# A shuffle taken out of one step into the next, and one weight difference moved from VectorE to GpSimd

## The chip, the cores and the metric

The kernel runs on one core of a Trainium2 chip. The time is the device time of that core in microseconds, as the median of several runs. The profile is of one execution of the program, taken by the hardware profiler.

## What is computed

An RWKV-6 attention over 4 batches, 8 heads, 768 tokens and a head size of 48, followed by a feed-forward layer with SiLU. All data is fp32.

```python
# r, k, v, w: (4, 8, 768, 48), u: (8, 48)
for t in range(S):
    kt, vt, rt, wt = (k[:, :, t], v[:, :, t], r[:, :, t], w[:, :, t])
    cur = np.einsum('bhd,bhe->bhde', u[None] * kt, vt)
    y[:, :, t] = np.einsum('bhd,bhde->bhe', rt, state + cur)
    state = wt[:, :, :, None] * state + np.einsum('bhd,bhe->bhde', kt, vt)
...
x = y.transpose(0, 2, 1, 3).reshape(B * S, H * D)     # (3072, 384)
h = x @ w_in                                          # w_in (384, 2048)
out = (h * (1.0 / (1.0 + np.exp(-h)))) @ w_out        # w_out (2048, 384)
```

## The kernel before

The work is cut into 12 units. A unit is 128 tokens of two batches (NB = 2); units 0 and 1 are the first 128 tokens of the four batches, units 2 and 3 the next 128, and so on. The order of all instructions is written out by hand: each engine has a queue that it works through in the order in which the program emits, and an engine that waits holds up all that is queued behind it.

**Attention of a unit.** The 128 x 128 scores of tokens against earlier tokens are built over seven levels l = 0 to 6. At level l, blocks of 2^l tokens meet their neighbours: `score_products` multiplies queries with keys on TensorE (L669), `keep_masked` (L679) copies the valid part from PSUM into `score` on VectorE, `grow_queries` (L607, VectorE) and `grow_keys` (L625, GpSimd) multiply queries and keys with the products of w for the next level. `prepare` (L737) makes queries for a next level in a second buffer ahead of time, so that `burst` can run two levels' products on TensorE at once: levels 3 and 4, later 5 and 6. The transposed inputs are made by `turn` (L360, VectorE), the products of w by `product` (L408, GpSimd) and a first growth of the keys by `grow_own` (L634, GpSimd).

**Scores within a block of 8.** From unit 3 on, the first three levels of scores are dot products made on GpSimd (`block_bonus`, L487) and summed on VectorE (`block_sum`, L521). `block_move` stores the sums in DRAM and loads them back with tokens on partitions (SP's queue, L540 and L543). `block_spread` copies them to `block_both` on ScalarE (L548, L550) and reverses the partitions of the second batch within groups of 32 on VectorE (L551, a stream shuffle in place). `block_write` (L557) copies `block_both` into `score` under a mask, twice on VectorE. Units 0 to 2 do the like for pairs of tokens with `bonus_spread` and `bonus_write` (L578, L584).

**Then** the keys are turned back (`turn_k`, L781), the state is applied (`y_state`, L794), the scores are applied to v (`y`, L807), and `update` renews the state: TensorE L821, GpSimd L826 (the old state times the decay), VectorE L835. `move_x` (L857) brings the result into the layout of the feed-forward layer by DMA.

**Feed-forward layer.** `up` multiplies with w_in (L925, 12 matmul records for each of 8 m) and applies SiLU on ScalarE (L934). Unit 0 uses a plain `down` (L947, copied out on VectorE by L951). From unit 1 on `down` is a fast 2 x 2 block product in seven quarters (`quarter`, L991, with additions on VectorE by L1000 that also free its PSUM buffers), which needs sums of the activations (`sums`, L973, VectorE: four operations for each of four m) and four differences of the weights, which `weight_sums` makes once: t1 = b12 - b11, t2 = b22 - t1, t3 = b22 - b12, and at last b21 = b21 - t2. The four quarters of w_out are 8 x 192 = 1536 elements on each of 128 partitions; t3 lies in `own[:, 2]` and is read by the quarter with number 3. The weight pieces that are put together at the start are added by GpSimd (L241).

**Order around the change.** For unit 2 the order is written out. Its part with `weight_sums(2)`:

```python
do((burst, 2, 5), (keep_level, 2, 5), (keep_level, 2, 6), (go_on, 2, 6), (up, 1, 6), (bonus_spread, 2), (bonus_write, 2),
   (load_values, 3), *both(turn_k, 2), (weight_sums, 2), (up, 1, 7), (sums, 1, 2))
do((sums, 1, 3), *both(y_state, 2), *both(y, 2), *both(update, 2), ...
```

On GpSimd the instruction before `weight_sums(2)` is thus the last of `grow_keys` in `go_on(2, 6)`, and the one after it the first of `update`. From unit 3 on, `mix` gives 13 groups of attention steps, and between the groups steps of `downs(i - 2)` and `ups(i - 1)` are put in. The groups that hold the block sums' last steps:

```python
[*at(first, *move), *at(later, (block_spread, i), (block_write, i))],
[(burst, i, 5), (keep_level, i, 5), *at(first, (block_spread, i)), (keep_level, i, 6), (go_on, i, 6),
 *at(first, (block_write, i))],
```

Here `first` is unit 3 and `later` the units 4 to 11. In unit 3 the spreading stands ahead of `keep_level(i, 6)` and `go_on(i, 6)` (which holds `grow_queries` of level 6), and the writing behind them.

Of the kernel before, what the change touches and what calls it, by code (L numbers as in the profile page):

```python
# [15 lines left out]
ALU = mybir.AluOpType  # L16
# [22 lines left out]
def kernel(  # L39
# [11 lines left out]
    nc = tc.nc  # L51
# [282 lines left out]
    for b in range(NB):  # L334
        for x in range(2):
            nc.vector.tensor_single_scalar(out=own_mask[:, b, :, x:x + 1], in_=first[0], scalar=tok[:, x, b:b + 1],
                                           op=ALU.is_equal)
# [118 lines left out]
    block_both = spare[:, at:at + NB * H * BLK].rearrange("p (b h s) -> p b h s", b=NB, h=H)  # L456
# [89 lines left out]
    def block_spread(i):  # L546
        flat = block_both.rearrange("p b h s -> p b (h s)")
        nc.scalar.copy(out=flat[:, 0], in_=block_diag[0])  # L548
        for g in range(4):
            nc.scalar.copy(out=flat[(3 - g) * 32:(4 - g) * 32, 1], in_=block_diag[1][g * 32:(g + 1) * 32])  # L550
        nc.vector.stream_shuffle(out=flat[:, 1], in_=flat[:, 1], mask=list(range(31, -1, -1)))  # L551

    def block_write(i):

        shape = [128, NB, NP, L // BLK, BLK]
        for e in range(2):
            nc.vector.copy_predicated(out=score[:, i % NSC, e].rearrange("p (b q) (i s) -> p b q i s", b=NB, s=BLK),  # L557
                                      mask=block_mask[:, :, None].to_broadcast(shape),
                                      data=block_both[:, :, e::2][:, :, :, None, :].to_broadcast(shape))
# [307 lines left out]
    def mix(i):  # L867
# [16 lines left out]
        def start(j):  # L884
# [11 lines left out]
                  [(keep_level, i, 4), (go_on, i, 4), *at(first, (make_block_mask,), *sum_steps(i, 2), *bonus_steps(i, 6))],  # L896
                  [(prepare, i, 5), (reverse_v, i), *at(first, *bonus_steps(i, 7))],
# [3 lines that stand above are left out]
                  [*at(later and ahead, *early)],  # L901
                  [*at(i < len(units) - NB, *both(turn_k, i)), *at(ahead, *turns(i + 1))],
# [59 lines left out]

    def weight_sums(which):
        out, one, two = ((t1, b12, b11), (t2, b22, t1), (t3, b22, b12), (b12, b21, t2))[which]
        nc.vector.tensor_tensor(out=out, in0=one, in1=two, op=ALU.subtract)

    def sums(i, m):

# [91 lines left out]
    for m in range(1, 4):  # L1060
# [11 lines left out]
              2: [(down, 0, 0, 1), (odd_ones, 2), (start_keys, 2, nc.gpsimd, True), (grow_queries, 2, 0), *blocks[3:6]],  # L1072
              3: [(up, 1, 3), (start_keys, 2, nc.gpsimd, False), (reverse_v, 2), *blocks[6:9]], 4: [(level, 2, 1), (up, 1, 4), *blocks[9:12]],
              5: [(down, 0, 0, 2), (up, 1, 5), (weight_sums, 0)]}
    for m in range(6):
        do((piece, 10 + m), *others[m])
    rounding.close()
    second.append(ctx.enter_context(tc.tile_pool(name="po", bufs=1, space=bass.MemoryType.PSUM)))

    blocks = block_loads(4)  # L1080
    do(*blocks[0:2], (level, 2, 2), (prepare, 2, 3), (weight_sums, 1), (down, 0, 1, 0), (down, 0, 0, 3), (down, 0, 1, 1),
       (sums, 1, 0), (bonus, 2, 0), (bonus_sum, 2, 0))
    do(blocks[2], (burst, 2, 3), (keep_level, 2, 3), (keep_level, 2, 4), (go_on, 2, 4), (prepare, 2, 5), (bonus, 2, 1),
       (bonus, 2, 2), (down, 0, 1, 2), (bonus_sum, 2, 1), (load_rk, 3), (load_u,), (sums, 1, 1), *blocks[3:7], (down, 0, 1, 3))
    do((burst, 2, 5), (keep_level, 2, 5), (keep_level, 2, 6), (go_on, 2, 6), (up, 1, 6), (bonus_spread, 2), (bonus_write, 2),
       (load_values, 3), *both(turn_k, 2), (weight_sums, 2), (up, 1, 7), (sums, 1, 2))
    do((sums, 1, 3), *both(y_state, 2), *both(y, 2), *both(update, 2),
       (move_x, 2),
# [47 lines left out]
```

## Time and profile before

| | us |
|---|---|
| median of 3 runs (lowest, highest) | 635.92 (635.87, 636.47) |
| the profiled execution, in all | 636.54 |
| its span | 634.8 |
| PE busy | 620.5 (98%) |
| PEld busy | 561.6 (88%) |
| DVE busy | 434.4 (68%) |
| POOL busy | 373.7 (59%) |
| ACT busy | 185.8 (29%) |

PE is TensorE's matmuls, PEld its weight loads, DVE VectorE, POOL GpSimd, ACT ScalarE, SP the queue that issues the DMAs. Starts are given in us from the begin of the span. The granted clock of TensorE is 0.997 of full speed in the profiled execution. A timeline line gives the start, the length, the engine, the source line, the operation with its output and inputs, the number of instructions merged, and in brackets the idle time of the engine ahead of it with what ended it.

### The profile page before, as it was taken

How to read it: one execution, taken by the hardware profiler on the slowest of the kernel's cores; microseconds unless marked ns; L12 is line 12 of the kernel's file. 1: busy time of each engine (PE TensorE's matmuls, PEld its weight loads, DVE VectorE, ACT ScalarE, POOL GpSimd, SP SyncE). 2: the span in 40 equal slices, each digit the busy share in tenths (PEclk: the TensorE clock that was granted, in tenths of full speed). 3: DMA queues.
4: the chain of work that ended last, by engine and by line, in shares of the span. 5: the costliest groups of instructions: out<-in, count | busy, mean ns of one | idle time of the engine just before them, and what ended most of it. 6: DMA issues, size and time to landing. Idle time of an engine off the chain costs nothing.

```text
span 634.8 us, 12253 instructions
## 1 busy us (share of the span) xinstructions
PE 620.5 (98%) x4574; PEld 561.6 (88%) x4574; DVE 434.4 (68%) x750; ACT 185.8 (29%) x377; POOL 373.7 (59%) x421
## 2 busy tenths in 40 slices
PE   8999999999888999999999999999999999999997
PEld 7888876889788899899889889989989989989997
DVE  7879779885593696696587596497597587561031
ACT  5798881202310321221221221221131122120120
POOL 6998298569469278478278378468458558500000
PEclk9999999999998999999999999999999999999999
DMA  9966864533353643543443442453353222100000
GB/s 216 290 152 167 190 176 50 112 73 65 81 71 55 128 65 52 126 64 51 111 67 52 110 72 49 96 87 51 79 102 53 47 62 52 34 0 26 26 1 25
DMA packets 203292, 53.75 MB, mean 85 GB/s; under 512 B 186465, under 2 KB 194657, under 8 KB 203233
## 3 DMA queue, kind: packets, MB, share of 16 engines
q1 hardware_dynamic: 201648, 52.39, 40.7%
q10 hardware_dynamic: 1584, 0.59, 0.5%
q8 instruction: 36, 0.59, 0.4%
q14 instruction: 24, 0.19, 0.1%
HBM read 43.67 MB, written 5.31 MB: 77 GB/s over the span
## 4 chain that ended last, share of the span: by engine, by line
PE 80%; POOL 9%; DMA 4%; DVE 3%; SPq 2%; issue 1%; ACT 1%; POOLq 0%; DVEq 0%; ACTq 0%
PE p_h L925 36%; PE p_o L991 27%; PE p_sc L669 4%; PE p_m L807 3%; PE p_m L947 2%; PE p_m L669 2%; PE p_m L794 2%; DMA tokens_w<-in_w_dram 2%; POOL ruk L487 2%; POOL tk L625 2%; POOL tw L408 2%; DMA u_bc<-in_u_dram 1%; POOL tk L634 1%; PE p_m L781 1%; PE p_sc L821 1%
## 5 line engine op out<-in xcount | busy, mean ns | idle before, releaser
L925 PE MATMUL p_h<-xt,w_in_sb 128*128 128x256 f32 x1152 | 258.1, 382 | 0.7 <-POOL tk L649 0.7
L925 PEld LDWEIGHTS p_h<-xt,w_in_sb 128*128 128x128 f32 x1152 | 215.9, 190 | 32.6 <-POOL tk L649 0.9
L934 ACT ACTIVATE gt<-p_h 128x512 f32<-128x512 f32 x90 | 53.6, 596 | 248.2 <-PE p_h L925 248.1
L625 POOL TENSOR_TENSOR tk<-tk,tw 128x256 f32<-128x256 f32 x126 | 86.9, 711 | 60.1 <-ACT tk L595 31.3
L991 PE MATMUL p_o<-own,temps 128*128 128x192 f32 x528 | 90.5, 331 | 5.8 <-DVE temps L1000 3.7
L991 PEld LDWEIGHTS p_o<-own,temps 128*128 128x128 f32 x528 | 87.6, 193 | 7.2 <-DVE temps L1000 4.6
L991 PE MATMUL p_o<-w_out_sb,gt 128*128 128x192 f32 x508 | 87.4, 328 | 0.0
L991 PEld LDWEIGHTS p_o<-w_out_sb,gt 128*128 128x128 f32 x508 | 82.7, 190 | 0.9 <-issue 0.4
L487 POOL TENSOR_TENSOR ruk<-tokens_rk 128x768 f32<-128x768 f32 (+1 forms) x36 | 56.3, 1574 | 39.4 <-DMA tokens_rk<-in_k_dram 28.2
L408 POOL TENSOR_TENSOR tw<-tw 128x256 f32<-128x256 f32 (+6 forms) x83 | 45.0, 542 | 52.2 <-DVE tw L360 48.3
L973 DVE TENSOR_TENSOR temps<-gt 128x256 f32<-128x256 f32 x84 | 54.7, 651 | 18.3 <-ACT gt L934 18.3
L595 ACT COPY tk<-tk 128x256 f32<-128x256 f32 x51 | 20.6, 403 | 101.6 <-POOL tk L625 71.9
L607 DVE TENSOR_TENSOR tr<-tr,tw 128x512 f32<-128x512 f32 x62 | 47.6, 768 | 3.7 <-POOL tk L625 1.1
L679 DVE COPY_PREDICATED score<-mask,p_sc 128x512 f32<-128x512 int8 x60 | 42.1, 753 | 10.9 <-PE p_sc L669 10.0
L669 PEld LDWEIGHTS p_sc<-tr,tk 48*128 48x128 f32 x496 | 30.4, 187 | 10.1 <-issue 6.6
L669 PE MATMUL p_sc<-tr,tk 48*128 48x128 f32 x496 | 36.5, 285 | 0.7 <-POOL tk L625 0.7
L521 DVE TENSOR_REDUCE block_sums<-ruk 128x4 f32<-128x192 f32 (+1 forms) x54 | 27.1, 542 | 7.5 <-POOL ruk L487 7.5
L1000 DVE TENSOR_TENSOR ob<-p_o,partial 128x192 f32<-128x192 f32 x22 | 7.9, 358 | 35.4 <-PE p_o L991 35.4
L1000 DVE TENSOR_TENSOR temps<-p_o,partial 128x192 f32<-128x192 f32 x22 | 7.9, 358 | 34.9 <-PE p_o L991 24.7
L557 DVE COPY_PREDICATED score<-spare 128x1024 f32<-128x1024 int8 x18 | 30.6, 1752 | 0.3
L991 PE MATMUL p_o<-w_out_sb,temps 128*128 128x192 f32 x176 | 30.4, 326 | 0.0
L487 POOL TENSOR_TENSOR tokens_rk<-tokens_rk,tokens_w 128x192 f32<-128x192 f32 (+1 forms) x36 | 29.4, 838 | 1.4
(170 smaller groups left out, 825.9 us busy)
## 6 DMA issues: line engine op xcount, KB each, us to landing
w_out_sb<-in_moe_w_in_dram SPq DMA_DIRECT2D x6, 768.0 KB, 8.1
tokens_rk<-in_r_dram SPq DMA_DIRECT2D x9, 384.0 KB, 4.5
tokens_rk<-in_k_dram SPq DMA_DIRECT2D x9, 384.0 KB, 5.5
tokens_w<-in_w_dram SPq DMA_DIRECT2D x9, 384.0 KB, 6.4
w_out_sb<-in_moe_w_out_dram SPq DMA_DIRECT2D x4, 768.0 KB, 6.8
own<-in_moe_w_out_dram SPq DMA_DIRECT2D x4, 768.0 KB, 5.2
xt<-yt SPq DMA_DIRECT2D x60, 48.0 KB, 2.0
raw<-in_w_dram SPq DMA_DIRECT2D x80, 32.0 KB, 2.4
```

The costliest lines, as they stand in the source:

```text
L408: engine.tensor_tensor(out=up, in0=t[:, :, 0::2], in1=t[:, :, 1::2], op=ALU.mult)
L487: mul = lambda out, one, two: nc.gpsimd.tensor_tensor(out=out, in0=one, in1=two, op=ALU.mult)
L521: add = lambda out, have: nc.vector.tensor_reduce(out=out, in_=have, axis=mybir.AxisListType.X, op=ALU.add)
L557: nc.vector.copy_predicated(out=score[:, i % NSC, e].rearrange("p (b q) (i s) -> p b q i s", b=NB, s=BLK), mask=block_mask[:, :, None].to_ ...
L607: nc.vector.tensor_tensor(out=odd, in0=odd, in1=tw[i][l][:, :, 0::2][:, :, :, None].to_broadcast([128, Q, L >> (l + 1), c]), op=ALU.mult)
L625: nc.gpsimd.tensor_tensor(out=out, in0=have, in1=odd_products(i, l, b, *blocks), op=ALU.mult)
L669: nc.tensor.matmul(bass.AP(tensor=s_p.tensor, offset=s_p.offset, ap=[s_p.ap[0], [apart * L // 2, 2], [1, L // 2]]), lhsT=tk[i][rows, X[l % ...
L679: nc.vector.copy_predicated(out=dst, mask=masks[l][:, :, None].to_broadcast([128, NB, NP, ni, c]), data=sc[e].rearrange("p (b q) (i c) -> ...
L925: nc.tensor.matmul(p_h[:, a, :], lhsT=w_in_sb[:, c, f * 128:(f + 1) * 128], rhs=xt[i][:, c, :], start=(c == 0), stop=(c == KC - 1))
L934: nc.scalar.activation(out=gt[i, m], in_=p_h, func=AF.Silu)
L973: nc.vector.tensor_tensor(out=out, in0=one, in1=two, op=op)
L991: nc.tensor.matmul(p, lhsT=left(f), rhs=right[:, f, :], start=(f == 0), stop=(f == FH - 1))
```

## The change

The stream shuffle is taken out of `block_spread` and put at the begin of `block_write`. The third call of `weight_sums` (which = 2, the difference t3) is issued to GpSimd, the other three stay on VectorE. Nothing is computed differently.

```diff
@@ block_spread, block_write
         nc.scalar.copy(out=flat[:, 0], in_=block_diag[0])
         for g in range(4):
             nc.scalar.copy(out=flat[(3 - g) * 32:(4 - g) * 32, 1], in_=block_diag[1][g * 32:(g + 1) * 32])
+
+    def block_write(i):
+
+        flat = block_both.rearrange("p b h s -> p b (h s)")
         nc.vector.stream_shuffle(out=flat[:, 1], in_=flat[:, 1], mask=list(range(31, -1, -1)))
-
-    def block_write(i):
 
         shape = [128, NB, NP, L // BLK, BLK]
         for e in range(2):
@@ weight_sums
     def weight_sums(which):
         out, one, two = ((t1, b12, b11), (t2, b22, t1), (t3, b22, b12), (b12, b21, t2))[which]
-        nc.vector.tensor_tensor(out=out, in0=one, in1=two, op=ALU.subtract)
+        (nc.gpsimd if which == 2 else nc.vector).tensor_tensor(out=out, in0=one, in1=two, op=ALU.subtract)
```

## The prediction

> **What bounds the kernel now.** I began with the busy times of the page, which say where to look for idle time:
>
> ```profile
> PE 620.5 (98%) x4574; PEld 561.6 (88%) x4574; DVE 434.4 (68%) x750; ACT 185.8 (29%) x377; POOL 373.7 (59%) x421
> ```
>
> TensorE is the bound of the whole, so an edit on another engine moves the end only through TensorE's few gaps. The timeline of PE from 95 to 250 us shows them (columns: start us, length us, what, and in brackets the idle time before it and its releaser):
>
> ```profile
> 137.35 5.47 PE L991 MATMUL p_o<-own,temps 128*128 128x192 f32 x32 [1.27 <-DVE temps L1000]
> ...
> 172.11 1.24 PE L781 MATMUL p_m<-ident,tk 128*128 128x128 f32 x8 [1.60 <-DVE score L679]
> ...
> 190.46 2.87 PE L991 MATMUL p_o<-own,temps 128*128 128x192 f32 x16 [2.00 <-DVE temps L1000]
> ...
> 195.43 4.55 PE L991 MATMUL p_o<-own,temps 128*128 128x192 f32 x16 [2.10 <-DVE partial L1000]
> ```
>
> Both edits lie ahead of these gaps; behind 195.43 the only gap noted up to 250 us is 0.45 us, and the chain of waits is PE almost alone. So **the time is set by when VectorE lets the product at 195.43 start**. Backwards from there: its buffer is freed by L1000 (195.03), queued behind L521 (193.60), which waits for GpSimd; GpSimd works from 179.75 to 193.53 with no idle noted, and began when VectorE had transposed w of unit 4 (L360, 178.37). VectorE has no idle between 171.12 and 190.05. One step further back, the timelines of DVE and then of POOL:
>
> ```profile
> 117.30 0.47 DVE L973 TENSOR_TENSOR temps<-gt,spare 128x256 f32<-128x256 f32 x1
> ...
> 118.82 0.55 DVE L951 COPY ob<-p_m 128x384 f32<-128x384 f32 x1
> ...
> 122.54 2.50 DVE L584 COPY_PREDICATED score<-own_mask,both_b 128x1024 f32<-128x1024 int8 x2
> 124.93 2.58 DVE L965 TENSOR_TENSOR own<-w_out_sb 128x1536 f32<-128x1536 f32 x1
> 127.44 1.25 DVE L973 TENSOR_TENSOR temps<-gt 128x256 f32<-128x256 f32 x1
> ...
> 132.33 1.30 DVE L360 STREAM_TRANSPOSE tw<-raw 128x512 f32<-128x512 f32 x2
> ...
> 171.12 0.22 DVE L551 STREAM_SHUFFLE spare<-spare 128x64 f32<-128x64 f32 x1
> 171.25 1.33 DVE L679 COPY_PREDICATED score<-mask,p_m 128x512 f32<-128x512 int8 x2
> 172.47 0.68 DVE L607 TENSOR_TENSOR tr<-tr,tw 128x512 f32<-128x512 f32 x1
> 173.07 2.49 DVE L557 COPY_PREDICATED score<-spare 128x1024 f32<-128x1024 int8 x2
> ```
>
> ```profile
> 116.30 1.19 POOL L625 TENSOR_TENSOR tk<-tk,tw 128x256 f32<-128x256 f32 x2
> 124.66 3.75 POOL L826 TENSOR_TENSOR state<-state,tw 128x512 f32<-128x512 f32 x2 [7.17 <-PE p_m L794]
> 133.72 1.04 POOL L408 TENSOR_TENSOR tw<-tw 128x512 f32<-128x512 f32 x1 [5.31 <-DVE tw L360]
> ```
>
> The reader is to see two places. At 171.12 the shuffle stands ahead of the keeping of level 6 (L679), though level 6's products are done at 165.06. At 133.72 GpSimd waits for VectorE (132.33), and from there to 164.05 GpSimd is busy with hardly a pause, up to the operand of the last block sum (L521, 164.09), whose DMA and ScalarE copies end in the shuffle at 171.12. A delay of VectorE at 132.33 therefore arrives at 171.12.
>
> **What the Trainium skill says.** "GPSIMD Engine Reference", section 3.1, gives 4497 ns for a GpSimd tensor_tensor of 2048 fp32 against 2293 ns on VectorE. The trace agrees: GpSimd takes 1.00 us for 384 elements and 1.82 for 768 (L487), 2.13 ns an element, hence 1.82 + 768 x 2.13 ns = **3.45 us for 1536** (estimate). "SBUF — State Buffer", section "SBUF: two separate sides", says that a VectorE operation with two SBUF inputs and a GpSimd operation that reads SBUF exclude each other for whole instructions. The trace agrees to 0.1 us: L826's first half ends at 125.90, L965, issued at 124.93, ends 1.61 later; the second half, issued at 125.86, ends 0.90 after that; L973, issued at 127.44, ends 0.28 after that. They take turns. Copies from PSUM are not held (L679 takes 0.7 us an instruction beside a running L487); the predicated copies with data in SBUF (L584) are, as L826's first half, 1.24 instead of 0.93, shows.
>
> **Edit 2, the difference t3 (L965, which = 2) on GpSimd.** It removes 2.58 us from VectorE (1.61 of work and a wait for L826) and adds 3.45 us to GpSimd between L625 and L826. GpSimd is idle there for 7.17 us, so its own queue loses nothing. But t3 is free to run at 117.49, when L625 ends, and just then VectorE has its run of L973 (sums, two SBUF inputs). Step by step:
> - The L973 that waits at 117.30 goes first, to 117.77 as now. t3 takes the ports from 117.7 to 121.1. The second L973 ends at 121.4 instead of 118.23: **+3.2** for all behind it on VectorE.
> - Behind it stands the copy L951, 119.37 + 3.2 = 122.6; it frees the PSUM buffer of TensorE's second key transpose, due at about 120.5, so TensorE waits some 2 us. Then L679 twice, the queries L607, and L584, which now begins at 125.74.
> - The state products on TensorE come at 125.65 instead of 123.53, so L826 is issued at about 126.7 and alternates with L584: L584 to 126.95, L826 0.93 to 127.9, L584 1.25 to 129.15, L826 to 130.05. L584 ends 4.1 later than 125.04. TensorE's y (125.41 now) needs the scores: 129.2, **+3.8** on TensorE.
> - Then, with L965 gone, L973 ends at 130.3, seven more at 0.37 give 132.9, L835 1.11 gives 134.05. L360 starts there instead of at 132.33: **+1.7** on the chain.
>
> TensorE's +3.8 meets the gap of 1.27 at 137.35 and leaves about 2.5; at 172.11 it meets 1.60 more and is 0.8 late, with 4.1 us of gaps (2.00 + 2.10) still ahead. It costs nothing at the end; without those gaps the 0.8 would be added. t3 is ready at 121 and first read at 137.
>
> **Edit 1, the shuffle.** No instruction is added; one of 0.22 us moves behind the keeping of level 6 and the queries L607. SP's, ScalarE's and GpSimd's queues pass nothing, the DMA order stays. Only unit 3 has work between the two places; in units 4 to 11 the writing follows the spreading at once, so nothing changes there. In unit 3 L679 and L607, 173.07 - 171.25 = **1.8 us**, run while the shuffle waits (4.83 us idle now), L557 follows the shuffle directly, and w's transposes come 1.8 earlier. TensorE's 1.60 gap goes as well; next it would wait for ScalarE (Silu at 170.99 behind the same copies), which is later than TensorE needs by little.
>
> **Sum.** Shuffle's data +1.7, w's transposes after it +1.7 - 1.8 = -0.1; GpSimd's chain to 193.53 and the product at 195.43 move by the same -0.1. The profiled execution has a span of 634.8 and 636.54 in all, 0.6 over the median of 635.92; the same -0.1 gives 635.8. The order at the port is uncertain by about 0.5 us at each of the two meetings, the saving by 0.3.
>
> **Rivals.**
> - *The sums get by (faster).* If VectorE's four L973 all pass before t3 gets the ports, t3 runs from 118.9 to 122.4 beside PSUM copies and holds only L607 by 0.7. VectorE then loses 0.7, saves about 1.3 of the 2.58 (the sums meet L826 instead), and w comes 0.6 earlier: -0.6 - 1.8 = -2.4, **633.5**. Against it: wherever both engines queue now, they alternate. For it: the first of the four is already waiting, and t3's dispatch is not in this trace.
> - *The saving is spent on a transfer (slower).* The chain of waits names a DMA of w, 177.13 to 178.98, just ahead of the second L360 at 179.00. If the transpose really waits for it, leaving VectorE earlier gives nothing, and since SP issues these loads behind the block sums' move, edit 2's +1.7 arrives in full: **637.6**. It decides from the moment VectorE is ready before the DMA lands. Against it: VectorE shows no idle there, and the blocks being loaded are those of unit 5, in the other half of the buffer.
> - *Neither meets anything:* an edit 2 that delays nothing and an edit 1 hidden anyway would also give no change; the place of the gaps would tell.
>
> **Chances.** About 0.2% (1.27 us) is what a measurement here can tell from no change. No change, with the sum of -0.1: 0.58. Faster 0.16. Slower 0.26: the transfer, or the port costing more than reckoned. The likeliest case alone spans 634.9 to 636.8; the range adds the slower rival whole and the upper part of the faster one's spread, and leaves out its 633.5: 634.0 to 637.8.
>
> **What would show it.** t3 on GpSimd at about 117.5, 3.5 us long; a L973 there of over 3 us; L951 ending near 122.6; y at 129; the first L360 of unit 3 near 134. Then L679 of level 6 before 170, the shuffle near 172.8 with L557 right behind it, the L360 of unit 4 near 178.3, and no PE gap at 172. An L973 of 0.42 us throughout, or an idle VectorE ahead of L360, would prove the sum wrong.

## The result and the profile after

| | before | both edits |
|---|---|---|
| median of 4 runs each | 636.0 us (635.87 to 636.47) | 637.29 us (637.12 to 639.4) |
| ratio, 95% interval | | 1.0027 (1.0005 to 1.0048) |
| measured again beside the experiments | 636.34 us (64 runs) | 637.58 us (19 runs), 1.0023 (1.0015 to 1.0032) |
| profiled execution, span | 634.8 us | 635.3 us |

The kernel became 1.2 to 1.3 us slower, by a quarter of a per cent. Line numbers after are two higher from `block_write` on (L967 is the weight difference, L975 the sums, L1002 the additions behind the quarters; the shuffle is now L555); in the experiments some are a few higher still. The profiled execution after runs 0.33 us ahead of the one before already at 95 us, where neither edit has acted: a GpSimd instruction begins at 94.93 instead of 95.27, and VectorE's reduction ahead of the sums at 116.04 instead of 116.38. Where this matters below, 0.33 is added to the difference, and that is said.

The timeline of DVE after, around the sums and then around the shuffle:

```profile
116.97 0.47 DVE L975 TENSOR_TENSOR temps<-gt,spare 128x256 f32<-128x256 f32 x1
117.47 3.54 DVE L975 TENSOR_TENSOR temps<-temps,gt 128x256 f32<-128x256 f32 x1
...
121.61 0.54 DVE L953 COPY ob<-p_m 128x384 f32<-128x384 f32 x1
...
125.31 2.50 DVE L586 COPY_PREDICATED score<-own_mask,both_b 128x1024 f32<-128x1024 int8 x2
...
133.32 1.30 DVE L360 STREAM_TRANSPOSE tw<-raw 128x512 f32<-128x512 f32 x2
...
167.22 1.32 DVE L681 COPY_PREDICATED score<-mask,p_m 128x512 f32<-128x512 int8 x2
168.44 0.67 DVE L609 TENSOR_TENSOR tr<-tr,tw 128x512 f32<-128x512 f32 x1
...
172.30 0.22 DVE L555 STREAM_SHUFFLE spare<-spare 128x64 f32<-128x64 f32 x1
172.56 2.50 DVE L559 COPY_PREDICATED score<-spare 128x1024 f32<-128x1024 int8 x2
```

GpSimd's side of the first part:

```profile
117.11 3.62 POOL L967 TENSOR_TENSOR own<-w_out_sb 128x1536 f32<-128x1536 f32 x1
```

One sum takes 3.54 us instead of 0.42: it is held for as long as t3 runs. Further on, keeping level 6 (L681) and the queries (L609) are done before 170, and the shuffle has the writing right behind it. Both edits do on VectorE what the prediction said. The surprise is in TensorE's gaps:

```profile
122.30 0.63 PE L783 MATMUL p_m<-ident,tk 128*128 128x128 f32 x4 [1.97 <-DVE ob L953]
127.87 0.96 PE L809 MATMUL p_m<-score,vt 128*48 128x128 f32 x13 [0.17 <-DVE score L586]
172.80 2.86 PE L927 MATMUL p_h<-xt,w_in_sb 128*128 128x256 f32 x12 [0.36 <-ACT gt L936]
189.95 2.87 PE L993 MATMUL p_o<-own,temps 128*128 128x192 f32 x16 [1.91 <-DVE temps L1002]
194.92 2.87 PE L993 MATMUL p_o<-own,temps 128*128 128x192 f32 x16 [2.10 <-DVE partial L1002]
...
244.55 5.47 PE L993 MATMUL p_o<-own,temps 128*128 128x192 f32 x32 [1.78 <-DVE temps L1002]
```

The product that was at 195.43 begins at 194.92, 0.5 sooner (0.2 with the offset), as forecast. But the next gap has grown from 0.45 to 1.78 us, and the product behind it begins at 244.55 instead of 243.97. From there to the end nothing changes: it starts 390.8 us ahead of the end of the span in both kernels. **The time is lost between 195 and 244**, in unit 4's stretch, where neither edit changes an instruction's place.

What is late there is read backwards: TensorE at 244.55 waits for VectorE's L1002, VectorE's queue leads back to unit 4's shuffle, this waits for ScalarE and the DMA of the block sums, and that for SP. SP's timeline before, and after it the same three lines of after:

```profile
165.07 0.33 SPq L540 DMA_DIRECT2D kept<-block_sums  x1
...
206.56 5.02 SPq L109 DMA_DIRECT2D raw<-in_w_dram  x8
...
212.63 0.42 SPq L540 DMA_DIRECT2D kept<-block_sums  x1
```

```profile
166.12 0.33 SPq L540 DMA_DIRECT2D kept<-block_sums  x1
...
208.49 3.85 SPq L109 DMA_DIRECT2D raw<-in_w_dram  x8
...
213.40 0.41 SPq L540 DMA_DIRECT2D kept<-block_sums  x1
```

The reader is to see two issues of L540, the block sums' move of unit 3 and of unit 4. Unit 3's moves by +1.05, since its sums come that much later with t3 on GpSimd. A move is a store and, some 2 us later, the loading back (L543); behind this SP issues load after load until unit 4's move, without a pause. That one is +0.77, although VectorE has unit 4's sums at 208.55, earlier than before (209.31). Unit 4's shuffle is +0.73 (218.63 to 219.36), w of unit 5 is transposed +0.59 later (230.53 to 231.12), the product near 244 +0.58.

The place where this delay gets into VectorE's queue is the keeping of unit 4's level 5, behind the writing. It needs TensorE's scores and, on VectorE, the end of the writing, which follows the shuffle. Before, and then after:

```profile
218.88 2.50 DVE L557 COPY_PREDICATED score<-spare 128x1024 f32<-128x1024 int8 x2
220.24 1.16 PE L669 MATMUL p_sc<-tr,tk 48*128 48x128 f32 x16
221.43 1.34 DVE L679 COPY_PREDICATED score<-mask,p_sc 128x512 f32<-128x512 int8 x2
```

```profile
219.48 1.16 PE L671 MATMUL p_sc<-tr,tk 48*128 48x128 f32 x16
219.62 2.50 DVE L559 COPY_PREDICATED score<-spare 128x1024 f32<-128x1024 int8 x2
222.01 1.32 DVE L681 COPY_PREDICATED score<-mask,p_sc 128x512 f32<-128x512 int8 x2
```

After, TensorE's scores come 0.76 us sooner, but the keeping waits for the writing: it begins 2.39 us behind the writing's begin. Before, it began 2.55 behind it and 1.19 behind TensorE's first product. So before, TensorE was the later of the two, by only about 0.15 us; of the shuffle's +0.73 this leaves the +0.58 that is found again at 244.

### The profile page after: what moved, and what is told of

The parts are those of the page before. It is cut to its first block, busy times and chain, and to the rows that moved or that the text cites. A ratio compares the mean times of both kernels' runs of the same rounds, so it can differ in the third digit from the quotient of the medians.

```text
span 635.3 us, 12254 instructions
## 1 busy us (share of the span) xinstructions
PE 619.6 (98%) x4574; PEld 560.3 (88%) x4574; DVE 433.1 (68%) x749; ACT 185.6 (29%) x377; POOL 376.8 (59%) x422
## 4 chain that ended last, share of the span: by engine, by line
PE 62%; DVE 2%; SPq 2%; DMA 2%; issue 1%; DVEq 0%
PE p_h L927 27%; PE p_o L993 26%; PE p_sc L671 3%; PE p_m L809 2%; PE p_m L671 2%; PE p_m L796 2%; SPq L109 1%; DMA tokens_w<-in_w_dram 1%; DVE temps L975 1%; PE p_m L783 1%; PE p_sc L823 1%; DVE block_sums L521 0%; DMA raw<-in_k_dram 0%; DMA kept<-block_sums 0%; DVE tr L609 0%
## 5 line engine op out<-in xcount | busy, mean ns | idle before, releaser
L993 PE MATMUL p_o<-own,temps 128*128 128x192 f32 x528 | 88.5, 327 | 5.8 <-DVE temps L1002 3.7
L993 PEld LDWEIGHTS p_o<-own,temps 128*128 128x128 f32 x528 | 86.0, 190 | 6.9 <-DVE temps L1002 4.3
L487 POOL TENSOR_TENSOR ruk<-tokens_rk 128x768 f32<-128x768 f32 (+1 forms) x36 | 57.8, 1616 | 41.6 <-DMA tokens_rk<-in_k_dram 30.3
L975 DVE TENSOR_TENSOR temps<-gt 128x256 f32<-128x256 f32 x84 | 54.6, 650 | 18.3 <-ACT gt L936 18.3
L681 DVE COPY_PREDICATED score<-mask,p_sc 128x512 f32<-128x512 int8 x60 | 42.0, 752 | 14.1 <-PE p_sc L671 13.5
L609 DVE TENSOR_TENSOR tr<-tr,tw 128x512 f32<-128x512 f32 x62 | 48.2, 778 | 3.7 <-POOL tk L627 1.1
L1002 DVE TENSOR_TENSOR ob<-p_o,partial 128x192 f32<-128x192 f32 x22 | 7.9, 357 | 35.0 <-PE p_o L993 34.9
L1002 DVE TENSOR_TENSOR temps<-p_o,partial 128x192 f32<-128x192 f32 x22 | 7.9, 357 | 34.9 <-PE p_o L993 24.7
L975 DVE TENSOR_TENSOR temps<-temps,gt 128x256 f32<-128x256 f32 x43 | 28.8, 670 | 1.5
```

Source lines behind the costliest of these rows:

```text
L487: mul = lambda out, one, two: nc.gpsimd.tensor_tensor(out=out, in0=one, in1=two, op=ALU.mult)
L609: nc.vector.tensor_tensor(out=odd, in0=odd, in1=tw[i][l][:, :, 0::2][:, :, :, None].to_broadcast([128, Q, L >> (l + 1), c]), op=ALU.mult)
L681: nc.vector.copy_predicated(out=dst, mask=masks[l][:, :, None].to_broadcast([128, NB, NP, ni, c]), data=sc[e].rearrange("p (b q) (i c) -> ...
L975: nc.vector.tensor_tensor(out=out, in0=one, in1=two, op=op)
L993: nc.tensor.matmul(p, lhsT=left(f), rhs=right[:, f, :], start=(f == 0), stop=(f == FH - 1))
```

## The experiments

Theory S says that SP's queue sets when unit 4 goes on. Theory V says that VectorE's chain of unit 3 alone sets the end, as the prediction reckoned. All comparisons are with runs of the kernel before on the same chip; an interval in us is the ratio's, times 636.3. The ratios are not those of the medians: where some executions are much longer than the rest, as in 2 to 4, they lie a little above these. At 116 us, ahead of all differences, the trace of experiment 1 stands 0.17 us behind that of before and that of experiment 2 0.18 ahead; this is not added below.

**1. Edit 1 alone.** The weight differences all stay on VectorE:

```diff
-        (nc.gpsimd if which == 2 else nc.vector).tensor_tensor(out=out, in0=one, in1=two, op=ALU.subtract)
+        nc.vector.tensor_tensor(out=out, in0=one, in1=two, op=ALU.subtract)
```

> Edit 1 alone; all four weight differences on VectorE. Theory S (SP's queue carries the delay): VectorE keeps its 1.8 us in unit 3, w of unit 4 is transposed 1.8 us sooner and the product near 195.4 starts about 1.7 sooner, but SP issues the block sums' move of unit 4 at 212.6 as before, the shuffle of unit 4 stays at 218.6, the gap ahead of the product at 244 grows from 0.45 to about 2.1 us, and the time stays at 636.0 (within 0.3). Theory V (VectorE's chain of unit 3 sets the end, as the prediction had it): the 1.8 arrives, 634.2.

Measured: 636.0 beside 636.34, ratio 0.9995 (0.9987 to 1.0003), no change. In the trace VectorE and TensorE do gain in unit 3: the product at 195.43 begins at 194.03. SP's second move stays at 212.66, and the gain turns into a gap of 1.36 us:

```profile
194.03 4.55 PE L993 MATMUL p_o<-own,temps 128*128 128x192 f32 x16 [2.10 <-DVE partial L1002]
243.48 5.47 PE L993 MATMUL p_o<-own,temps 128*128 128x192 f32 x32 [1.36 <-DVE temps L1002]
```

1.4 us were gained at 195 and 0.5 is left at 244. Theory S holds; that the gap is 1.36 and not 2.1 is because the gain at 195 was 1.4 and not 1.7, and unit 4's shuffle came 0.4 sooner with the same time on SP.

**2. Edit 2 alone.** The shuffle as in the kernel before, t3 on GpSimd.

> Edit 2 alone; the shuffle stays where it was. Theory S: the block sums' move of unit 3 is issued 1.0 to 1.4 us later, SP is late by that up to the move of unit 4 at about 213.5, and the end comes as late as with both edits, 637.0 to 637.4. Theory V: both edits together minus edit 1's gain, so 1.8 us slower than both edits: about 639.

Measured: 637.91, ratio 1.0029 (1.0021 to 1.0037), +1.3 to +2.4 us. Between the two forecasts. SP's second move is +0.98 (213.61), but the product at 195.43 is itself at 196.78, +1.35, and the gap near 244 stays at 0.46. Here SP is not what holds unit 4: behind the writing VectorE waits 0.84 us for TensorE's scores and keeps level 5 at 222.78, 1.19 behind TensorE's first product as in the kernel before. It is the delay of VectorE's and TensorE's own chain, 1.35, that arrives. So theory S as written is too narrow: **the end follows the later of two chains**, VectorE's and TensorE's from unit 3, and SP's. In the kernel before they are within some 0.15 us of each other. Edit 1 takes 0.3 us off edit 2 by the medians (637.91 to 637.58; the intervals overlap), not 1.8.

**3. SP's queue alone.** Two of unit 5's loads are issued a second time between the two moves:

```diff
+        if i == NPAIR:
+            loads.insert(4, (load_again, i + NSLOT))
```

> The kernel before, with two of unit 5's loads of w issued a second time on SP between unit 3's and unit 4's move of the block sums (the same data to the same place, some 1.25 us of SP's issuing). No instruction of VectorE, GpSimd, ScalarE or TensorE is changed. Theory S: unit 4's shuffle comes about 1.2 us later, the gap of 0.45 ahead of the product at 244 grows to about 1.5, and the time is 637.0 to 637.3. Theory V: no change, 636.0.

Measured: 637.08, ratio 1.0016 (1.0008 to 1.0024), +0.5 to +1.5 us. The product at 195.45 has not moved, SP's second move is at 213.37 (+0.74, the two loads took 0.94), the shuffle of unit 4 at 219.12, the gap near 244 grew from 0.45 to 0.89. A delay on SP and on nothing else lengthens the kernel. That the added transfers get in the way of others does not show here: from the move to the shuffle it takes 5.75 us, 6.00 before. The trace shows 0.5 us at the product near 244, the runs 0.7 by the medians and 1.0 by the ratio, with an interval that holds all three.

**4. Both edits again.**

> Both edits, measured again beside the others. Theory S: 637.0 to 637.3, with unit 4's move on SP at 213.4 and a gap of about 1.8 us ahead of the product at 244.5. Theory V: the same as before within 0.3 us, its first slower runs being chance.

Measured: 637.58, ratio 1.0023 (1.0015 to 1.0032); SP's second move at 213.44, a gap of 1.05 us, less than forecast, ahead of the product at 244.63. The loss is no chance.

**5 to 7. The block sums' move brought forward on SP.** In unit 4 its loads for unit 6 are spread over groups 6 to 12, so that eight of them no longer stand ahead of the move (which is in group 5):

```diff
-        behind = groups[3 if i > NTOK + 1 else 10:]
+        behind = groups[3 if i > NPAIR + 1 else 6 if i == NPAIR + 1 else 10:]
```

With the kernel before:

> The kernel before, with unit 4's loads of unit 6 spread over its groups 6 to 12 instead of 3 to 12, so that eight loads of w no longer stand ahead of the block sums' move on SP. Theory S: the move is issued when VectorE has the sums (about 209.5 instead of 212.6), the shuffle of unit 4 comes some 2 to 3 us sooner, the gap of 0.45 ahead of the product at 244 goes, and the time falls by 0.4: 635.9 beside 636.3. If something else held VectorE in unit 4, no change.

With edit 1 alone:

> Edit 1 with that spreading of the loads; no difference on GpSimd. Theory S: what edit 1 gains in unit 3 (1.4 us at the product near 195) now arrives, and the gap near 244 of 1.4 us is gone: 634.4 to 634.6, 1.8 under the kernel before. Theory V as it stands now (edit 1's gain lost elsewhere): 636.0 as with edit 1 alone.

With both edits:

> Both edits with that spreading of the loads. Theory S: the gap near 244 of 1.1 to 1.8 us goes, the two edits cancel as the prediction summed them, 635.7 to 636.0, 0.3 to 0.6 under the kernel before. If the loss of both edits lies elsewhere: 637.5.

Measured: 635.78 with the kernel before (0.9996, 0.9988 to 1.0004, no change that can be told), **634.19 with edit 1 (0.9970, 0.9959 to 0.9980)**, and 635.79 with both edits (0.9997, 0.9988 to 1.0005). SP issues the move at 208.64, 207.71 and 210.71, and in none of the three is a gap left near 244 (the trace with both edits is of the longest of its 13 executions, 637.22 us). Edit 1's gain, lost in experiment 1, arrives: 1.6 us between the first two. It shows where level 5 of unit 4 is kept: edit 1 brings this forward by 0.54 us with the loads as they were (221.43 to 220.89), by 1.43 with the loads spread (220.74 to 219.31). And with both edits the cost of edit 2 and the gain of edit 1 cancel, as the prediction's sum had it (635.79 beside 635.78).

The spreading does one thing more. The loads for GpSimd's dot products of unit 5 (L139) stand right behind the move, so they come sooner too, and GpSimd is done with most of that work before VectorE's eight sums of unit 4: these take 3.75 us in all three kernels, 6.05 in the kernel before and 6.06 with both edits. By the traces it is this, and not the earlier shuffle, that closes the gap of 0.45 with the kernel before: level 5 is kept 26.0 us behind the product at 195 with the loads spread and without. Both effects go over SP's queue; in the loss of the two edits only the first is at work, since the sums took the same time before and after. The lines of edit 1 with the loads spread: first SP, then all gaps of PE from 190 to 634 us:

```profile
164.75 0.33 SPq L540 DMA_DIRECT2D kept<-block_sums  x1
207.71 0.41 SPq L540 DMA_DIRECT2D kept<-block_sums  x1
```

```profile
193.56 2.87 PE L993 MATMUL p_o<-own,temps 128*128 128x192 f32 x16 [0.43 <-DVE partial L1002]
197.59 2.87 PE L993 MATMUL p_o<-w_out_sb,gt 128*128 128x192 f32 x16 [1.16 <-DVE partial L1002]
```

**8. What holds the sums.** Both edits, with t3 left out: GpSimd clears its room twice instead, which writes and reads nothing.

```diff
+        if which == 2:
+            for x in range(2):
+                nc.gpsimd.memset(own[:, 2], 0)
```

> Both edits, but t3 is not computed: in its place GpSimd clears that room twice (two memsets of 1536 words, some 1.4 us each), so that it is busy as before and reads nothing. Port theory (only an instruction of GpSimd that reads excludes VectorE's two-input ones): no sum is held, L975 takes 0.42 us throughout from 117.5 to 119, the copy L953 ends near 119, no PE gap at 122, and w of unit 3 is transposed at about 131. Rival (GpSimd busy at all holds VectorE): an L975 of 1.5 to 3 us remains.

Measured: 634.21, ratio 0.9973 (0.9962 to 0.9983). GpSimd is busy for 2.82 us from 117.39, and no sum is held:

```profile
117.76 0.43 DVE L979 TENSOR_TENSOR temps<-temps,gt 128x256 f32<-128x256 f32 x1
...
118.78 0.55 DVE L953 COPY ob<-p_m 128x384 f32<-128x384 f32 x1
```

w of unit 3 is transposed at 130.50 instead of 132.33. So GpSimd's being busy and writing does not hold VectorE; what t3 does beyond that is to read two inputs from SBUF. Without this, taking L965 off VectorE is worth 1.8 us on its chain. The run also bears on SP: the loads are as they were, unit 3's move is issued 1.77 us sooner than before (163.30) and unit 4's 1.85 sooner (210.78). **From the one move to the other SP takes 47.3 to 47.6 us in all six traces with the loads as they were** (before, after, experiments 1, 2, 4 and 8), and 48.3 with the two loads of experiment 3. So what unit 3's sums gain here arrives without any spreading of the loads, because SP's run begins sooner too.

**9 and 10. t3 behind the sums.** By experiment 8 and the prediction's reading that copies from PSUM are not held, t3 should run while VectorE copies from PSUM (L953 and four L681, 3.0 us). An addition of one element ahead of t3 that reads the last sum makes it start there:

```diff
+        if which == 2:
+            last = quarters[:, 3, 2, 0:1]
+            nc.gpsimd.tensor_tensor(out=shift, in0=last, in1=last, op=ALU.add)
```

> Both edits and the spreading of the loads, and a one-element addition on GpSimd ahead of t3 that reads the last of the four sums, so that t3 starts behind them, beside VectorE's copies from PSUM. Port theory: no L975 is held ahead of the copy L953 (ends near 119.5), only the queries L609 by about 0.7, w of unit 3 is transposed about 1 us sooner than before (131.2), and the time is 0.8 to 1.2 us under the kernel with edit 1 and the spreading: about 633.2. If the order at the port goes against it (a later instruction held for 3 us): 635 to 636.

Beside it, edit 1 with the loads spread once more:

> Edit 1 with the spreading of the loads, again, beside the run with t3 behind the sums: 634.2, 2.1 us under the kernel before.

Measured: **633.16, ratio 0.9957 (0.9944 to 0.9969)**, beside 634.24 (0.9968, 0.9956 to 0.9980) for edit 1 with the loads spread and 636.31 before. t3 begins at 119.49, and one instruction is held by it, by the 0.7 us expected:

```profile
118.85 0.42 DVE L978 TENSOR_TENSOR temps<-spare,temps 128x256 f32<-128x256 f32 x1
119.18 0.55 DVE L953 COPY ob<-p_m 128x384 f32<-128x384 f32 x1
...
122.11 1.39 DVE L609 TENSOR_TENSOR tr<-tr,tw 128x512 f32<-128x512 f32 x1
```

```profile
119.34 0.19 POOL L969 TENSOR_TENSOR shift<-temps 128x1 f32<-128x1 f32 x1 [1.49 <-DVE temps L978]
119.49 3.45 POOL L970 TENSOR_TENSOR own<-w_out_sb 128x1536 f32<-128x1536 f32 x1
```

The two intervals overlap, so that t3 behind the sums is better by 1.1 us is a difference of medians, not one that is clear of noise; that both beat the kernel before (by 0.3 to 0.4%) is.

## Why the prediction was wrong

It forecast no change (635.8, 0.1 under the median shown); the kernel is 0.2 to 0.3% slower. The measured time lies in the stated range, on the side that was given 0.26.

- **t3 on GpSimd, 3.45 us and held sums: right.** 3.62 us from 117.11, the second sum held to 121.01, L953 at 122.15 (122.6 forecast), TensorE's wait of 1.97 for it (some 2).
- **L584 held by L826: wrong, and too large.** L826 was forecast at the port ahead of the second predicated copy. After, the copies (L586) ran from 125.31 to 127.81 and took some 1.3 us each, so the second had just begun when L826 (now L828) was issued at 126.54. It was L828 that waited, 3.32 us for its two, and the copies ended at 127.81 instead of 129.15. y on TensorE came at 127.87 (129.2 forecast), and w of unit 3 +1.0 later, +1.3 with the offset of 0.33, where the sum had +1.7.
- **Edit 1, 1.8 us: right.** The shuffle is +1.5 and w of unit 4 -0.2 (177.87 for 178.37), both with the offset: 1.7 between them.
- **The sum of -0.1 up to the product at 195.43: right,** -0.2 with the offset, in part by luck: edit 2's cost was put 0.4 too high at w of unit 3 and 0.2 too high at the shuffle, and 0.1 was missing from edit 1's gain. (TensorE's remainder at 172.11 is 0.9 by the prediction's own numbers, 2.5 less 1.60, not 0.8; nothing hung on it.)
- **The step that failed** is the one that carried this sum to the end: "behind 195.43 the only gap noted up to 250 us is 0.45 us, and the chain of waits is PE almost alone", together with "SP's, ScalarE's and GpSimd's queues pass nothing, the DMA order stays", which was said of edit 1 and left edit 2's delay of SP at nothing. Behind 195.43 one chain was reckoned, and there are two: unit 4's keeping of level 5 also waits for the shuffle, which is released over SP, and in the kernel before this one was level with TensorE's scores within 0.15 us. The order on SP stays, but its run of loads starts with unit 3's move and has no slack until unit 4's. So edit 2's delay of unit 3's sums (+1.05 on SP) reaches unit 4 over SP (+0.77), past VectorE, where edit 1 can't give it back, and arrives at the product near 244 as +0.58. Experiment 3 shows the coupling by itself, experiments 5 to 7 that it is the term that was missing: with it removed, the kernel with both edits stands at 0.9997 of the one before, the forecast. The gap of 0.45 itself did not give it away: in experiment 2 it moved along unchanged, as the prediction had taken it.
- **Of the rivals,** the slower one saw that loads issued behind the block sums' move carry edit 2's delay in full, but put it at the wrong place: w of unit 4 did not wait for a transfer (VectorE has no idle between the shuffle and L360 there), the block sums of unit 4 did. The faster one named what experiment 9 then made happen.

How the 1.2 us of the runs divide is open in part. The traces account for 0.6 (0.9 with the offset) at 244.55. Part of the rest lies in single long executions: in experiments 2, 3 and 4, in which SP issues unit 4's move latest (213.37 to 213.61), 10 of 21, 2 of 22 and 5 of 19 took 638.4 us or more, and one of the four with both edits in the first table; none of the 64 of the kernel before and none of any other experiment did. Without them the medians would be 0.7 to 0.9 us above the kernel before, about what the traces show. What these executions lose beyond that is open, since no trace is of one of them. Most show a granted clock of 0.995 or less; but executions of the kernel before at 0.994 and 0.995 are no longer than 637.61, so the clock alone does not explain it.

## What to carry to other kernels

When a bound engine shows a small gap behind the place of a change, follow it back, and ask at each step what else could have released that instruction: here the way leads to a copy on VectorE for which a second chain, over the DMA queue, was ready only 0.15 us ahead of the first, and only the later of the two counts. A queue that issues without a pause has a pace of its own, here 47.3 to 47.6 us from one move to the next: what delays the first issue of the run delays all of them, and a gain on a compute engine can't overtake it. When an operation is given to GpSimd, look at what VectorE does in the same microseconds: beside copies from PSUM t3 held one instruction for 0.7 us, beside two-input sums it held the queue for 3.1.

## What was not expected of the hardware

Experiment 8 bore out what it had forecast: GpSimd instructions that only write (two memsets of 1536 words, 2.82 us) did not hold VectorE's two-input sums (0.42 to 0.43 us each), while one of 3.62 us with two SBUF inputs held one of them to its end. Not forecast was the order at the other meeting. Which of two instructions comes first at such a meeting is worth about a microsecond here: L828, issued just behind the begin of a predicated copy, left VectorE's pair of copies at 2.50 us, and the y behind them came 1.3 us (1.0 with the offset) sooner than with the order that the prediction had reckoned; that order itself was not run.
